# DeltaNet and a low-rank token mixer in one kernel: the low-rank products on smaller tiles of TensorE, with a new table of ranks

## The chip, the cores and the metric

The kernel runs on one core of a Trainium2 chip. The metric is the device time of one execution in microseconds (us); lower is better. The core has five engines with queues of their own: TensorE (PE in the profile; PEld is its weight load), VectorE (DVE), ScalarE (ACT), GpSimd (POOL) and SyncE (SP), which here only issues transfers.

## The reference

Two layers follow each other. The first is a delta-rule recurrence over 768 tokens for 4 batches and 8 heads of size 48. Its output, with the heads side by side (384 columns), is the x of the second, a mixer with a low-rank product over the tokens and a two-layer product over the channels.

```python
k_n = k / (np.linalg.norm(k, axis=-1, keepdims=True) + 1e-06)
for t in range(S):
    y[:, :, t] = np.einsum('bhd,bhde->bhe', q[:, :, t], state)
    v_old = np.einsum('bhde,bhd->bhe', state, kt)
    state = state + bt[:, :, :, None] * np.einsum('bhd,bhe->bhde', kt, vt - v_old)
...
xt = x.transpose(0, 2, 1)
h = xt @ U @ V
u = x + h.transpose(0, 2, 1)
ch = np.maximum(u @ w_ch1, 0.0) @ w_ch2
return (u + ch).astype(np.float32)
```

U is 768 x 32, V 32 x 768, w_ch1 384 x 1536, w_ch2 1536 x 384. U, V and the two weights come as 64-bit floats and are turned into 32-bit ones on the chip; everything else is fp32.

## The kernel before, in words

**The recurrence.** Each batch is cut in two units of 6 chunks of 64 tokens (units n = 0 to 7). For a unit, q and k are loaded and turned on TensorE (L646 with full 128x128 transposes, or L420 with 64x64 matmuls against the identity), multiplied with each other (L673), and a triangular system per chunk and head is solved: VectorE does a substitution (L758, L764) on blocks laid out by transposes (L749, L771), and TensorE joins the blocks (L814, L828, L854 to L875). The products L973 and L984 prepare a unit. Then `recur` goes through the chunks of a batch: L1022 applies the state, VectorE subtracts (z, L1035), L937 and L951 make the output y, which ScalarE copies to X (L921), and L1050 makes the change of the state, which VectorE adds (s, L1060). Each of these steps on TensorE is a group of eight small matmuls.

**The weights** are decoded on VectorE (L1155 to L1183) in 14 slices, two of them U and V, from staging space that lies partly in X and hs. V stands four times in v_sb, once in each quarter of the partitions.

**The mixer.** `front(b, i)` is called for each batch b and each third i of its tokens (256). For i = 0 it makes tt = U^T x (L1346): the six 128-token blocks of x are multiplied by U's blocks on four column tiles of 32, so that tt holds four partial sums of 384 columns in its four quarters of partitions; VectorE copies it out (L1352). For each i it then makes V^T tt (L1364), one 128x128 matmul of 384 columns for each 128-token block, which also adds up the four quarters; VectorE adds it to X (L1368), TensorE turns the result (L1387 or L420), and ScalarE copies it to ut (L1390). `wide(b, i)` holds the first product over the channels in six groups (`channels`, L1447, six matmuls of 256 columns), each with a relu on ScalarE (L1412), and the second as seven products of six matmuls (`narrow`, L1562), whose results VectorE gathers into X (L1487). The last batch makes its first product in another way (`quick`, L1251).

**The order of the work** is not written by hand. Every part is a generator that yields the operations it wants to do, with an estimated cost and a mode, and the keys it needs (`need`) or gives (`emitted`). `run` keeps a model of the engines' clocks and always emits next the operation that could start first, in case of a tie the one with the lower rank. The ranks are the table PLACES: "channels b0 i1 e4 84.16" is the rank of one part. An entry that ends in "quad 1" allows a part a second form. The instructions are emitted in that order; hardware waits are added for what they read and write.

**Modes.** "F" is a matmul on the full 128x128 array, "Q" four 64x64 tiles (QUADS), "T" column tiles of 32, "J" 32x32 tiles. A part with two forms takes "Q" only when its quad entry is there and the array is in that mode already. In the Q form a channel group takes both PSUM banks of `mix`, of which the full form takes one, and goes in two halves: `crossed` (L408) emits four 64x64 matmuls for two outputs, and between the halves `swap` has ScalarE read one column of each bank (L417). Two products of `narrow` can be paired in the same way.

The piece that makes the Q form:

```python
def crossed(jobs):
    for r, g in QUADS:
        to, w, x, start, stop = jobs[r]
        nc.tensor.matmul(
            to[half(g)], w[half(r), half(g)], x[half(r)],
            start=start, stop=stop, skip_group_check=True,
        )
```

Of the kernel before, what the change touches and what calls it, by code (L numbers as in the profile page):

```python
# [8 lines left out]
FP32 = mybir.dt.float32  # L9
# [6 lines left out]
L = 64  # L16
# [10 lines left out]
def kernel(  # L27
# [115 lines left out]
    add_up b0 i0 76.06; add_up b0 i1 10; add_up b0 i2 92; add_up b1 i0 94.5; add_up b1 i1 -57.95  # L143
    add_up b1 i2 13.5; add_up b2 i0 4.89; add_up b3 i0 119.12; add_up b3 i1 17.69; add_up b3 i2 2.95
    blocks n1 83.63; blocks n2 19.95; blocks n3 96.74; blocks n4 107.02; blocks n5 204.56; blocks n6 121.16
    blocks n7 126.66; both 73; channels b0 i0 e0 96.95; channels b0 i0 e1 105.6; channels b0 i0 e2 -27.57
    channels b0 i0 e3 129.38; channels b0 i0 e4 91.95; channels b0 i0 e5 71.15; channels b0 i1 e0 25
    channels b0 i1 e1 19.03; channels b0 i1 e2 34; channels b0 i1 e3 5.2; channels b0 i1 e4 84.16
    channels b0 i1 e5 30.5; channels b0 i2 e0 52; channels b0 i2 e1 46.94; channels b0 i2 e2 75.56
    channels b0 i2 e3 116.36; channels b0 i2 e4 51.09; channels b0 i2 e5 99.28; channels b1 i0 e0 113.65  # L150
    channels b1 i0 e1 91.5; channels b1 i0 e2 53.98; channels b1 i0 e3 100.61; channels b1 i0 e5 120.34
    channels b1 i1 e0 128.05; channels b1 i1 e1 30.85; channels b1 i1 e2 104.15; channels b1 i1 e3 58.65
    channels b1 i1 e4 15.5; channels b1 i1 e5 91.65; channels b1 i2 e0 118.43; channels b1 i2 e1 -2.08
    channels b1 i2 e2 73.28; channels b1 i2 e3 -8.98; channels b1 i2 e4 111.65; channels b1 i2 e5 32.87
    channels b2 i0 e0 38.24; channels b2 i0 e2 4.5; channels b2 i0 e3 127.92; channels b2 i0 e4 22.75
    channels b2 i0 e5 95.78; channels b2 i1 e0 274.53; channels b2 i1 e1 94; channels b2 i1 e2 97.16
    channels b2 i1 e3 91.59; channels b2 i1 e4 73; channels b2 i1 e5 1.09; channels b2 i2 e0 28.09
    channels b2 i2 e1 44.19; channels b2 i2 e2 57.06; channels b2 i2 e3 68.5; channels b2 i2 e4 73
    channels b2 i2 e5 9.5; copies 56.49; cut 75.73; diagonals n0 h0 19.22; diagonals n0 h1 62.5
    diagonals n1 h0 52; diagonals n2 h0 15.5; diagonals n2 h1 94.5; diagonals n3 h0 32; diagonals n3 h1 93.24  # L160
    diagonals n4 h0 7.5; diagonals n4 h1 95.58; diagonals n5 h0 33.96; diagonals n5 h1 27; diagonals n6 h0 92.63
    diagonals n6 h1 -0.5; diagonals n7 h0 88.94; diagonals n7 h1 69.62; first 30.4; front b0 i0 -7.49
    front b0 i0 quad 1; front b0 i1 75.5; front b0 i1 quad 1; front b0 i2 -10.38; front b1 i0 71.77
    front b1 i1 76; front b1 i1 quad 1; front b1 i2 73.06; front b2 i0 4.43; front b2 i0 quad 1; front b2 i1 12.82
    front b2 i1 quad 1; front b2 i2 68.32; front b2 i2 quad 1; front b3 i1 -1.47; front b3 i2 94.5
    gather b0 i0 h0 c0 77.72; gather b0 i0 h0 c1 16.74; gather b0 i0 h1 c0 -15; gather b0 i1 h0 c0 -18.11
    gather b0 i1 h0 c1 -19.16; gather b0 i1 h1 c0 111.34; gather b0 i1 h1 c1 99.53; gather b0 i2 h0 c0 109.5
    gather b0 i2 h0 c1 36.92; gather b0 i2 h1 c0 4.78; gather b0 i2 h1 c1 84.78; gather b1 i0 h0 c0 21.21
    gather b1 i0 h1 c0 79.5; gather b1 i0 h1 c1 103.91; gather b1 i1 h0 c0 92.5; gather b1 i1 h0 c1 122.8
    gather b1 i1 h1 c0 101.5; gather b1 i2 h1 c0 77.08; gather b1 i2 h1 c1 45; gather b2 i0 h0 c0 13.32  # L170
    gather b2 i0 h0 c1 82.99; gather b2 i0 h1 c0 124.83; gather b2 i0 h1 c1 3.53; gather b2 i1 h0 c0 80.62
    gather b2 i1 h0 c1 73.95; gather b2 i1 h1 c0 80.36; gather b2 i1 h1 c1 76.58; gather b2 i2 h0 c0 95.84
    gather b2 i2 h1 c0 25.35; gather b3 i0 h0 c0 2.88; gather b3 i0 h0 c1 113; gather b3 i0 h1 c1 113
    gather b3 i1 h0 c0 -4; gather b3 i1 h0 c1 23.12; gather b3 i1 h1 c0 44.69; gather b3 i1 h1 c1 28.1
    gather b3 i2 h0 c0 105.1; gather b3 i2 h0 c1 37.88; gather b3 i2 h1 c0 109.03; gather b3 i2 h1 c1 92.38
    grams n0 i0 54.5; grams n0 i1 5; grams n1 i0 -5.73; grams n1 i1 16.5; grams n2 i0 64.85; grams n2 i1 5.5
    grams n3 i0 10.25; grams n4 i0 140.55; grams n4 i1 0; grams n6 i1 103.46; grams n7 i0 120.26
    grams n7 i1 124.04; joins n0 h1 42; joins n1 h0 -10.78; joins n1 h1 90.6; joins n2 h0 46.2; joins n2 h1 -9.38
    joins n3 h0 18.36; joins n3 h1 -3; joins n4 h0 49.57; joins n4 h1 108.36; joins n5 h0 6.33; joins n5 h1 -4.95
    joins n6 h1 102.05; joins n7 h0 91.09; joins n7 h1 -26.22; last_sum b0 i0 107.65; last_sum b0 i1 -0.5  # L180
    last_sum b0 i2 58; last_sum b1 i0 6.24; last_sum b1 i1 90.99; last_sum b1 i2 72.32; last_sum b2 i0 -3.27
    last_sum b2 i1 94.5; last_sum b3 i1 76.04; last_sum b3 i2 90; load n0 namek halves(0,) -2.13
    load n0 namek halves(1,) 6.19; load n0 nameq halves(0,) 89.12; load n0 nameq halves(1,) 77.79
    load n0 namev halves(0,) 106; load n0 namez halves(0,) 113.97; load n0 namez halves(1,) 7.5
    load n1 namek halves(0,) 81.07; load n1 namek halves(1,) 73.91; load n1 nameq halves(0,) 43.57
    load n1 nameq halves(1,) 91.1; load n1 namev halves(0,) 27.89; load n1 namev halves(1,) 70.76
    load n1 namez halves(0,) 93.39; load n1 namez halves(1,) 5.01; load n2 namek halves(0, 1) 29.55
    load n2 nameq halves(0, 1) 67.61; load n2 namev halves(0, 1) 60.56; load n2 namez halves(0, 1) 107.23
    load n3 namek halves(0, 1) 11; load n3 nameq halves(0, 1) -4.84; load n3 namev halves(0, 1) 66.59
    load n3 namez halves(0, 1) 25.89; load n4 namek halves(0, 1) 65.35; load n4 nameq halves(0, 1) 24.5  # L190
    load n4 namev halves(0, 1) 81; load n4 namez halves(0, 1) 30.74; load n5 namek halves(0, 1) 109.5
    load n5 nameq halves(0, 1) 92; load n5 namev halves(0, 1) 38.85; load n5 namez halves(0, 1) -21.49
    load n6 namek halves(0, 1) 32.5; load n6 nameq halves(0, 1) 37.61; load n6 namev halves(0, 1) 7.15
    load n6 namez halves(0, 1) 62; load n7 namek halves(0, 1) 95; load n7 nameq halves(0, 1) 1.5
    load n7 namez halves(0, 1) 47.39; load_beta u0 45.5; load_beta u1 29.9; load_weights 107.15
    narrow b0 i0 e0 56.12; narrow b0 i0 e0 quad 1; narrow b0 i0 e1 123.3; narrow b0 i0 e2 71.6
    narrow b0 i0 e3 101.43; narrow b0 i1 e0 41.5; narrow b0 i1 e0 quad 1; narrow b0 i1 e2 81.41
    narrow b0 i1 e3 118.5; narrow b0 i1 e3 quad 1; narrow b0 i2 e0 92.51; narrow b0 i2 e1 88.93
    narrow b0 i2 e2 -54.32; narrow b0 i2 e2 quad 1; narrow b0 i2 e3 94.65; narrow b1 i0 e0 45.5
    narrow b1 i0 e0 quad 1; narrow b1 i0 e1 90.54; narrow b1 i0 e1 quad 1; narrow b1 i0 e2 16.95  # L200
    narrow b1 i0 e3 14.03; narrow b1 i1 e0 93.52; narrow b1 i1 e1 44.39; narrow b1 i1 e3 98
    narrow b1 i1 e3 quad 1; narrow b1 i2 e0 99.1; narrow b1 i2 e0 quad 1; narrow b1 i2 e1 30.56
    narrow b1 i2 e2 62; narrow b1 i2 e2 quad 1; narrow b1 i2 e3 0.76; narrow b2 i0 e0 108.5
    narrow b2 i0 e1 135.19; narrow b2 i0 e2 56.93; narrow b2 i0 e3 42.7; narrow b2 i1 e0 quad 1
    narrow b2 i1 e1 -11.39; narrow b2 i1 e2 109.47; narrow b2 i1 e2 quad 1; narrow b2 i1 e3 quad 1
    narrow b2 i2 e0 86.52; narrow b2 i2 e0 quad 1; narrow b2 i2 e1 92.56; narrow b2 i2 e2 106.1
    narrow b2 i2 e3 quad 1; narrow b3 i0 e0 95.5; narrow b3 i0 e1 66.42; narrow b3 i0 e1 quad 1
    narrow b3 i0 e2 24; narrow b3 i0 e2 quad 1; narrow b3 i0 e3 80.5; narrow b3 i1 e0 102.5; narrow b3 i1 e1 70.08
    narrow b3 i1 e2 1; narrow b3 i2 e0 48.87; narrow b3 i2 e1 58; narrow b3 i2 e1 quad 1; narrow b3 i2 e2 55.62
    narrow b3 i2 e2 quad 1; narrow b3 i2 e3 97.45; norms n0 68.5; norms n1 -53.8; norms n2 30.5; norms n3 110.41  # L210
# [1430 lines left out]
```

## Time and profile before

| | |
|---|---|
| median of 3 runs | 618.48 us (618.42 to 619.09) |
| span of the profiled execution | 612.3 us |
| what lies around the span (median less span) | 6.2 us |
| TensorE busy | 582.1 us, 10824 matmul records |
| VectorE busy | 417.3 us, 1000 instructions |
| ScalarE busy | 236.6 us |
| GpSimd busy | 98.4 us |
| U products start (L1346) | 109.8, 240.5, 377.6, 488.7 us |
| first matmul of the last batch's own first product (L1251) | 524.1 us |

The profile is one execution, seen from the first to the last instruction; its own time is the span and what lies around it, and by the median of the runs that is 618.5 us. An fp32 matmul leaves two records on TensorE, a transpose one. TensorE's matmuls overlap, so the mean length of one (243 ns for the small ones) is not its price: that is the length of a group in the chain of work divided by its matmuls. The clock of a stretch is the share of the full TensorE clock that was granted in it. Stages are told here from one U product to the next.

### The profile page before, as it was taken

To read this page: it belongs to the slowest core of one execution; us is meant where nothing else is said; L and a number is where in the kernel's file an instruction comes from. 1 tells how busy PE (TensorE), PEld (TensorE's weight loads), DVE (VectorE), ACT (ScalarE), POOL (GpSimd) and SP (SyncE) were. 2 spreads that over 40 slices of the span, in tenths; PEclk is the share of its full clock that TensorE was granted. 3 is DMA by queue.
4 is the path that set the end of the run, shared out by engine and by line. 5 is a ranking of instruction groups with operands and counts; after the bars stand their busy time and mean duration, and the time that the engine had idled before them with its cause. 6 is when DMAs were issued, how large, how long until landed. Compare 5 with 4: busy or idle time off the path is not lost.

```text
span 612.3 us, 24053 instructions
## 1 busy us (share of the span) xinstructions
PE 582.1 (95%) x10824; PEld 502.3 (82%) x10824; DVE 417.3 (68%) x1000; ACT 236.6 (39%) x466; POOL 98.4 (16%) x169
## 2 busy tenths in 40 slices
PE   4798887999999999999999999999999999999997
PEld 4788786688989987988889988978989889656997
DVE  5998899898899348988895888287843223332542
ACT  3645666255412652265218224253163220344000
POOL 8321050520004304110043002220010000000000
PEclk9655557799999999999999999999999999999999
DMA  9911686940006205200071002310000000000000
GB/s 142 163 42 55 209 193 169 137 130 19 3 28 98 67 4 91 61 16 3 4 123 42 16 16 53 74 42 4 28 3 3 29 2 1 26 2 0 16 36 27
DMA packets 63847, 33.31 MB, mean 54 GB/s; under 512 B 50816, under 2 KB 61824, under 8 KB 63744
## 3 DMA queue, kind: packets, MB, share of 16 engines
q1 hardware_dynamic: 56800, 23.21, 17.6%
q0 software_dynamic: 5344, 8.27, 6.5%
q8 instruction: 85, 1.39, 0.9%
q10 hardware_dynamic: 1600, 0.30, 0.3%
q14 instruction: 18, 0.15, 0.1%
HBM read 27.03 MB, written 4.72 MB: 52 GB/s over the span
## 4 chain that ended last, share of the span: by engine, by line
PE 83%; DVE 11%; issue 2%; ACT 2%; POOL 1%; DMA 1%; DVEq 0%; ACTq 0%; POOLq 0%
PE P L1562 25%; PE P L1447 24%; PE P L1251 7%; PE P L673 3%; PE P L408 3%; PE P L1364 2%; PE P L646 2%; PE P L1022 2%; PE P L973 2%; PE P L1050 2%; PE P L984 2%; PE P L951 2%; DVE prod L758 2%; PE P L937 2%; DVE xt L764 2%
## 5 line engine op out<-in xcount | busy, mean ns | idle before, releaser
L1447 PE MATMUL P<-ut,w_sb 128*128 128x256 f32 x648 | 151.6, 385 | 0.1
L1447 PEld LDWEIGHTS P<-ut,w_sb 128*128 128x128 f32 x648 | 119.4, 190 | 18.2 <-issue 1.2
L1562 PE MATMUL P<-w_sb,hs 128*128 128x192 f32 x468 | 82.4, 330 | 0.2 <-ACT hs L1412 0.2
L1562 PEld LDWEIGHTS P<-w_sb,hs 128*128 128x128 f32 x468 | 75.9, 190 | 2.0 <-ACT hs L1412 0.3
L764 DVE TENSOR_TENSOR xt<-xt,prod 128x112 f32<-128x112 f32 (+21 forms) x200 | 64.6, 323 | 6.9
L758 DVE TENSOR_TENSOR prod<-gs,xt 128x112 f32<-128x112 f32 (+21 forms) x200 | 64.0, 320 | 4.4
L1487 DVE TENSOR_TENSOR X<-X,P 128x192 f32<-128x192 f32 x84 | 29.3, 351 | 53.5 <-PE P L1562 50.7
L1412 ACT ACTIVATE hs<-P 128x512 f32<-128x512 f32 x54 | 32.3, 597 | 82.9 <-PE P L1447 73.6
L921 ACT COPY X<-P 64x192 f32<-64x192 f32 x96 | 30.0, 313 | 80.7 <-PE P L951 74.0
L1562 PE MATMUL P<-w_sb,S 128*128 128x192 f32 x264 | 45.9, 328 | 0.0
L1562 PEld LDWEIGHTS P<-w_sb,S 128*128 128x128 f32 x264 | 42.9, 190 | 1.2 <-DVE X L1487 0.6
L531 POOL DMA_DIRECT2D slot<-in_k_dram x44 | 29.1, 671 | 64.3 <-PE P L1050 64.2
L646 PE MATMUL P<-ident,slot 128*128 128x128 f32 x192 | 30.8, 309 | 8.2 <-DMA slot<-in_k_dram 8.1
L673 PE MATMUL P<-slot 48*64 48x64 f32 x1536 | 32.8, 243 | 4.8 <-ACT slot L660 4.8
L893 ACT COPY slot<-zz 32x384 f32<-32x384 f32 x64 | 32.5, 508 | 9.1 <-DVE zz L832 4.9
L673 PEld LDWEIGHTS P<-slot 48*64 48x64 f32 x1536 | 29.4, 155 | 7.9 <-ACT slot L660 6.0
L646 PEld LDWEIGHTS P<-ident,slot 128*128 128x128 f32 x192 | 25.0, 158 | 11.7 <-issue 8.7
L1251 PE MATMUL P<-slot,w_sb 128*128 128x384 f32 x96 | 33.2, 486 | 0.0
L1562 PE MATMUL P<-w_sb,slot 128*128 128x192 f32 x180 | 30.6, 327 | 0.9 <-DVE X L1487 0.9
L660 ACT COPY slot<-P 128x768 f32<-128x768 f32 x30 | 23.5, 796 | 20.1 <-PE P L646 18.0
L1562 PEld LDWEIGHTS P<-w_sb,slot 128*128 128x128 f32 x180 | 29.4, 190 | 2.0 <-DVE X L1487 1.5
L531 POOL DMA_DIRECT2D slot<-in_q_dram x32 | 21.0, 664 | 56.8 <-ACT X L921 40.5
(150 smaller groups left out, 935.9 us busy)
## 6 DMA issues: line engine op xcount, KB each, us to landing
out_dram<-X SPq DMA_DIRECT2D x22, 192.0 KB, 1.9
X<-in_moe_w_ch_dram SPq DMA_DIRECT2D x10, 384.0 KB, 3.9
wide<-in_moe_w_ch_dram SPq DMA_DIRECT2D x10, 384.0 KB, 4.4
slot<-in_k_dram SPq DMA_DIRECT2D x48, 72.0 KB, 4.8
slot<-in_k_dram POOLq DMA_DIRECT2D x44, 72.0 KB, 4.8
slot<-in_q_dram SPq DMA_DIRECT2D x32, 72.0 KB, 4.4
slot<-in_q_dram POOLq DMA_DIRECT2D x32, 72.0 KB, 4.7
slot<-in_v_dram SPq DMA_DIRECT2D x32, 72.0 KB, 3.4
```

What stands on the lines that cost most here:

```text
L531: queue.dma_start(out=t[half(1 - g if name == "z" else g), :, to, 0:D], in_=src[b, 4 * g + s, hf * UC * L : (hf + 1) * UC * L, :].rearrang ...
L646: nc.tensor.transpose(p_t[:, c // 3, c % 3], t[:, c, 2 * j : 2 * j + 2].rearrange("p s d -> p (s d)"), ident,)
L673: nc.tensor.matmul(p_g[half(g ^ (par * i)), par, c], kq[rows, c, j, 0, half(g)], kq[rows, c, j, i, half(g)], start=True, stop=True,)
L758: nc.vector.tensor_tensor(out=prod, in0=gb[:, :, j : j + 1, j + 1 :].to_broadcast([128, split, m, w]), in1=xb[:, :, 0:m, j : j + 1].to_bro ...
L764: nc.vector.tensor_tensor(out=xb[:, :, 0:m, j + 1 :], in0=xb[:, :, 0:m, j + 1 :], in1=prod, op=ALU.subtract,)
L893: nc.scalar.copy(pg[quarter(i), :, at, :, a : a + BK], cut(zc, h)[quarter(i)].rearrange("p r (c j) t -> p r c j t", j=2),)
L921: nc.scalar.copy(x[half(c % 2), c // 2, 4 * D * g : 4 * D * (g + 1)].rearrange("p (j r d) -> p r j d", r=2, d=D), states(p_y)[half(g)],)
L1251: nc.tensor.matmul(to, w, t, start=start, stop=stop, skip_group_check=True)
L1412: nc.scalar.activation(hs[:, fs[0] : fs[1] + 1 : fs[1] - fs[0]], p_f, ACTF.Relu)
L1447: nc.tensor.matmul(p_f[:, x], w(x, t), ut[:, t], start=(t == 0), stop=(t == KT - 1))
L1487: nc.vector.tensor_tensor(out=to, in0=to, in1=p, op=ALU.add)
L1562: nc.tensor.matmul(to, of[0], of[1], start=of[2], stop=of[3], skip_group_check=True)
```

## The change

U^T x goes on the four column tiles in another division: two tiles take the left half of the columns and two the right half, one of each pair the even token blocks and one the odd ones, so there are 12 matmuls of 192 columns and tt has 192 columns. In tt, the upper 64 partitions then hold two partial sums of the left half and the lower 64 those of the right. The V product follows that: for each token block four 64x64 tiles of 192 columns, over 64 rows each, in place of one 128x128 matmul of 384 columns. The addition to X reads its halves from two PSUM banks.

In the planner the modes and costs of the two operations are those of the new forms (U product 0.98 and 48 words, V product 0.66, "Q" and 32 words). New keys are needed: a load into a unit's space needs the last state product of the unit two before (`used`), the second copy of beta rows the first transposed betas, the copies of y to X the end of what was staged there (beta in batch 0; weight slices 12 and 13 in batch 1), and the first batch's relu slice 7, which was staged in hs.

PLACES is a new table: 607 entries in place of 511, 17 of them unchanged. It has 78 quad entries in place of 37; those of `channels` (35) are new. In the order of instructions that results, 14 of the 54 channel groups and 2 pairs of second products have the Q form, where it was none and 4; 170 changes of mode become 154.

```diff
     PLACES = """
...
-    channels b0 i0 e3 129.38; channels b0 i0 e4 91.95; channels b0 i0 e5 71.15; channels b0 i1 e0 25
...
+    turn n5 i1 j1 nameq 113.93; turn n5 i1 j1 nameq quad 1; turn n6 i0 j0 namek 94.9; turn n6 i0 j0 namek quad 1
...
-        yield need(("rec", n - 2), *[("x", b - 1, UC * hf + c) for c in range(UC)])
+        yield need(("rec", n - 2), ("used", n - 2), *[("x", b - 1, UC * hf + c) for c in range(UC)])
...
         rows = beta_rows
+        yield need(("betas", 0)) if u else []
...
         def put(c, y, p_y):
-            yield need(("stored", b - 2, c // 2)) if b > 1 else []
+            yield need(("stored", b - 2, c // 2)) if b > 1 else need(
+                ("beta", 1) if b == 0 else ("freed", W2 + 4) if c < 8 else ("weights", W2 + 5)
+            )
...
+                if cu == UC - 1:
+                    emitted(("used", n))
                 yield op("dve", dve(192), give=[("pair", xs)])
...
+            else:
+                emitted(("used", n))
...
         if i == 0:
-            o = yield op("pe", 1.3, "T", take="pair", words=24)
-            p_t = one(o)[:, 0:DM]
-            for c in range(NB):
-                nc.tensor.matmul(
-                    p_t[R * (c % 4) : R * (c % 4) + R], u_sb[:, c], x[:, c],
-                    start=(c < 4), stop=(c + 4 >= NB),
-                )
-            yield op("dve", dve(384), give=[("pair", o)])
-            tts[b] = mix.tile([128, DM], FP32, name="tt", bufs=1)
+            o = yield op("pe", 0.98, "T", take="pair", words=48)
+            p_t = one(o)[:, 0:HD]
+            for c in range(0, NB, 2):
+                for k in range(4):
+                    nc.tensor.matmul(
+                        p_t[quarter(k)], u_sb[:, c + k % 2],
+                        x[:, c + k % 2, HD * (k // 2) : HD * (k // 2) + HD],
+                        start=(c == 0), stop=(c + 2 == NB),
+                    )
+            yield op("dve", dve(HD), give=[("pair", o)])
+            tts[b] = mix.tile([128, HD], FP32, name="tt", bufs=1)
             nc.vector.tensor_copy(out=tts[b], in_=p_t)
...
-        o = yield op("pe", 1.3, "F", take="pair", words=8)
-        p_h = pair(o)[:, :, 0:DM]
+        o = yield op("pe", 0.66, "Q", take="pair", words=32)
+        p_h = pair(o)[:, :, 0 : NT * HD].rearrange("p r (m d) -> p r m d", m=NT)
         for m, c in enumerate(cs):
-            nc.tensor.matmul(
-                p_h[:, m], v_sb[:, c * 128 : (c + 1) * 128], tt, start=True, stop=True
-            )
+            for r, g in QUADS:
+                nc.tensor.matmul(
+                    p_h[half(g), r, m],
+                    v_sb[half(r), c * 128 + L * g : c * 128 + L * g + L],
+                    tt[half(r)],
+                    start=True,
+                    stop=True,
+                )
         yield op("dve", dve(768), give=[("pair", o)])
-        nc.vector.tensor_tensor(out=x[:, at], in0=x[:, at], in1=p_h, op=ALU.add)
+        to = x[:, at].rearrange("p m (r d) -> p r m d", r=2)
+        nc.vector.tensor_tensor(out=to, in0=to, in1=p_h, op=ALU.add)
...
         def relu(fs, ms, p_f):
+            yield need(("freed", W2 - 1)) if b == 0 else []
             yield op("act", act(2 * GT), give=[("mix", m) for m in ms])
```

## The prediction

> **What bounds the kernel now.** I read the page's head and slices first, then the busy time by stretch, then the chain of work in order of time, and last the timeline around one of the rare quarter-array products.
>
> ```profile
> span 612.3 us, 24053 instructions
> ...
> PE 582.1 (95%) x10824; PEld 502.3 (82%) x10824; DVE 417.3 (68%) x1000; ACT 236.6 (39%) x466; POOL 98.4 (16%) x169
> ...
> DVE  5998899898899348988895888287843223332542
> ...
> PEclk9655557799999999999999999999999999999999
> ...
> PE 83%; DVE 11%; issue 2%; ACT 2%; POOL 1%; DMA 1%; DVEq 0%; ACTq 0%; POOLq 0%
> ```
>
> TensorE is busy for 95% of the span and has 83% of the chain. The first 105 us are different: VectorE is at nine tenths, and TensorE runs at half clock.
>
> ```profile
> 75.00:90.00 15.00, 13.37 (x465) 12.32 (x469) 14.16 (x26) 9.75 (x21) 6.93 (x12) 0.56 0.80 195
> 90.00:105.00 15.00, 10.40 (x367) 8.86 (x364) 14.80 (x27) 9.84 (x17) 1.29 (x3) 0.84 0.78 194
> ...
> 150.00:200.00 50.00, 49.98 (x899) 45.40 (x899) 45.27 (x114) 15.42 (x31) 6.88 (x11) 1.00 0.23 41
> ...
> 350.00:400.00 50.00, 49.93 (x759) 43.34 (x758) 33.27 (x82) 16.93 (x35) 7.78 (x12) 1.00 0.20 44
> ```
>
> (Columns: stretch, length, then TensorE, weight loads, VectorE, ScalarE, GpSimd with counts, granted clock, DMA.) From 150 us on TensorE has no idle time and clock 1.00: what leaves its queue there leaves the total. Prices come from the chain in order of time (start, length, line, records; an fp32 matmul leaves two records, a transpose one):
>
> ```profile
> 240.48 1.42 PE P L1346 x12
> 241.89 1.49 PE P L1447 x6
> 243.38 1.29 PE P L1364 x4
> ...
> 300.50 0.99 PE P L408 x24
> ...
> 430.10 0.71 PE P L420 x48
> ...
> 494.89 1.30 PE P L1447 x6
> ```
>
> L1447 is 1.29 to 1.30 us inside a run of full-array work and 1.49 when it is the first after another tile shape: a change of shape costs 0.20 in this direction and 0.15 in the other (L673, x48: 0.86 after full-array work, 0.71 otherwise). I take 0.175 for each.
>
> **The change, part by part.** The profiled execution's span is 612.3 us; the median of the runs is 618.5, so 6.2 us lie around the span, and I keep these. The sum is made against 612.3 and 6.2 together, which is the median.
>
> *U^T x.* Before, 6 matmuls of 384 columns on four column tiles: 1.42 with its change of shape, 1.29 without, two rounds of 0.645 (L1364's matmul of the same 384 columns). After, 12 matmuls of 192 columns, three full rounds. L408 moves 12 quarter-array matmuls of 192 columns in 0.99, so three rounds are 0.98. Four times 0.31 is -1.2 us. The tt copy has half the columns (0.56 to about 0.35 on VectorE, four times); in the TensorE-bound stages this hides under the channel or product groups next in the queue.
>
> *V product.* Before, 2 matmuls of 384 columns, 1.29. After, 8 quarter-array matmuls, two rounds of 192: 0.65 by the same row. Twelve times 0.64 is -7.7 us. The addition to X keeps its 768 elements (L1368, 0.95): nothing.
>
> *New ranks.* They decide order and form. I compared the order in which the instructions of the two kernels stand. Matmul totals are equal but for forms: 14 of 54 channel groups (none before) and 2 pairs of the second product (4 before) are in quarter-array form. A form costs the same: 24 quarter matmuls of 256 columns are six rounds of 0.43, which six full ones take too. After the first U product 18 full transposes fewer, at 0.109 each (-2.0), stand against 48 quarter ones more, at 0.71 per 24 (L420: +1.4). Changes of shape there go from 139 to 125: -14 x 0.175 = -2.4.
>
> *Check of these prices.* I sum each stage of the queue (three channel matmuls 1.29, six second products 1.95, quick 0.645 a matmul, a recurrence group of eight 0.235, 24 products 0.71) from one U product to the next. Before this gives 129.7, 137.1, 108.3 and 35.5 us; the trace has 130.7, 137.1, 111.1 and 35.4 (U products at 109.8, 240.5, 377.6, 488.7, first quick matmul at 524.1). The prices hold. The changed order gives 132.7, 122.3, 122.6 and 21.1: 398.7 against 410.6, or -11.9. The last batch is the same list of matmuls in both.
>
> *Ahead of the first U product* VectorE sets the pace: 106.8 us of its work stand ahead of the first tt copy, which began at 112.6. The changed order puts 106.1 there. SP and GpSimd queue the same transfers; GpSimd's memset of xt moves ahead of four q loads, and three v loads behind the next memset, which waits for VectorE (L771, 27.6). Four loads took 2.6 us to issue and 3.5 to land, so these land near 36.4, where L610 read them at 36.6. Nothing, within a microsecond.
>
> *Waits written down.* Most hold a load, a copy out of PSUM or a relu behind work that stands far ahead: weights 7 and 12 are decoded at 92 and 140 us, before the first relu needs the one and the second batch's x the other. A load that now also waits for the last state product of the unit two before waited for that unit's outputs already; the next loads and stores stand behind it on SP and GpSimd, and only transposes of a later unit wait for them. Nothing; if the cover went, a load's 4.8 us to land would be seen.
>
> *What the quarter form adds.* Between the halves of such a group TensorE waits for a ScalarE read (L417). The timeline of one of the four that existed:
>
> ```profile
> 468.31 0.44 PE L1022 MATMUL P<-s,slot 48*64 48x48 f32 x12
> ...
> 468.65 0.16 ACT L417 COPY seen<-P 128x2 f32<-128x2 f32 x1 [2.48 <-PE P L408]
> 468.86 0.37 PEld L408 LDWEIGHTS P<-w_sb,hs 64*64 64x64 f32 x12
> ```
>
> From leaving the first half (468.31) to the second (468.86): 0.55, with two recurrence groups (0.47) in it, 0.08 open. Nine of the 14 have just two such groups there: about 1.0 in all. A quarter channel also takes both banks that full channels alternate in, so the relu before it (L1412, 0.60) must end first: at 371.5 TensorE left a channel and re-entered both banks 0.74 later, behind three groups. In seven places of the new order one or two groups stand there: 1.6 together. Bounds: 0 if all is covered, 14 x (0.68 + 0.75) = 20 if nothing is. I take 2.6, since I can count the cover.
>
> The Trainium skill, TensorEngine Tiling (Array Packing), Performance Considerations (PSUM Bottleneck), says that tiling speeds up TensorE but not the emptying of PSUM, which may become the limit. By it the sum would lie toward the upper bound, at 629; the four pairs in this trace, 0.08 open in the one shown, speak for the lower, near 611.
>
> *Stage after the first U product.* There VectorE is near. I sum VectorE's work from the first tt copy and TensorE's from the first U product up to the places where one needs the other: where TensorE reads the second batch's first z, its sum was 3.9 us ahead of VectorE's before and is 0.3 now; at the first matmul (L854) on unit 3's solved blocks it was 7.1 and is 2.9. In addition the first V product has no filler behind the tt copy, and a quarter channel follows the first turned x with ScalarE's 0.80 copy in between. Bounds 0 (before showed no TensorE idling in 150 to 200) and 3.6 (all the slack lost). I take 2.0. Instruction fetches: TensorE's records go from 21648 to 23004, five more of the 256-record packets of which queue q8 moved 85; TensorE stood once for 1.3 us (L872, "issue") between two of these. I take 0.3 of 0 to 1.3.
>
> Sum: 618.5 - 11.9 + 2.6 + 2.0 + 0.3 = 611.5.
>
> **Rivals.**
> *All covered.* The new waits hide, and the 2.8 us that stage three lost before (111.1 against 108.3) may be saved too: 606.6, at best 603.8. For: TensorE idled under 1 us in most stretches. Against: 14 new halting points.
>
> *VectorE binds the first mixed stage.* It has 116.7 us of work between first and second tt copy, 108.3 before, in 129.4 us. With the same 21.1 idle it needs 137.8, where my stage has 134.7: 614.6. For: the slack of 0.3. Against: part of that idling was waiting for TensorE.
>
> *Slower: quarter channels held by both banks.* Place: L408's channel groups, their L417 read and L1412 relu. Price up to 1.43 each, 629 at full. From 0.7 us open per group (618.5 less 608.9, over 14) the kernel is slower. Against: the order puts recurrence work in each gap. For: nine gaps are covered by 0.47 only, and ScalarE's 0.31 copies may stand ahead of the read.
>
> *The tiles don't overlap.* If V's eight matmuls ran one after another (0.33 each) they would cost 2.6, not 0.65: 611.5 + 23 = 635. L408's 24 records in 0.99 speak against it.
>
> **How the numbers follow.** Chances: forecast 0.43, all covered 0.27, VectorE-bound 0.11, slower by held banks 0.12, no overlap 0.02, no measurable change 0.05 (several of the costs at half). A difference of 0.2% (1.2 us) is about what a measurement can tell from no change. Faster gets 0.43 + 0.27 + 0.11 = 0.81; same 0.05; slower 0.14. The predicted time is the forecast's, 611.5. The range 604.5 to 619 takes in the first three cases and leaves out the slower ones and a little below.
>
> **What would show it.** U groups of 0.98 us and V groups of 0.65 in the chain; TensorE near 570 us busy; L417 with 16 copies and under 0.3 us idle of TensorE around each; TensorE still without idle in 150 to 200. Wrong if L408 or the groups next to it wait on ScalarE for more than 0.7 each, if the first U product comes after 113 us, or if V's groups take over 1 us.

## The result: faster by 3 to 4 us, where 7 were forecast

The changed kernel has a median of 614.53 us (611.88 to 617.45, 12 runs), the kernel before 618.22 us (615.05 to 619.09, 12 runs). The ratio is 0.9955, with an interval of 0.9934 to 0.9976. The forecast was 611.5 us: the direction and the range held, the size did not. By the medians the gain is 3.7 us, by the ratio 2.8 (1.5 to 4.1), where 7.0 were forecast. That the range held says little: it ended at 619 and so took in a kernel that had not changed at all (618.5).

The first lines of the page of the changed kernel: span, busy time of the engines, slices of VectorE and of the granted clock, and the chain by engine.

```profile
span 610.2 us, 25422 instructions
...
PE 571.3 (94%) x11502; PEld 497.0 (81%) x11502; DVE 417.4 (68%) x1000; ACT 237.1 (39%) x478; POOL 98.4 (16%) x169
...
DVE  4999897898998528898887388869852124332542
...
PEclk9976556799999999999999999999999999999999
...
PE 82%; DVE 10%; ACT 3%; issue 3%; DMA 1%; ACTq 0%; DVEq 0%
```

TensorE is busy for 10.8 us less, as its lists of matmuls said it would be (near 570). But the span is only 2.1 us shorter, and this execution took 611.88 us, 1.7 more than its span. In every later profile it is 1.6 to 2.0 (617.0 for a span of 615.3, 609.64 for 607.9). So the profiled execution of before, with a span of 612.3, took about 614.0 by estimate. It was a quick one, and the 6.2 us "around the span" were mostly the distance from it to the median. I therefore cut the spans in two, and profiled the kernel before once more.

| us | first U product starts | from there to the end | U to U, U to U, U to U, U to quick, quick to end |
|---|---|---|---|
| before | 109.7 | 502.6 | 130.7, 137.1, 111.1, 35.3, 88.4 |
| before, second profile | 113.6 | 501.7 | 130.1, 137.1, 110.8, 35.3, 88.4 |
| changed | 115.3 | 494.9 | 135.7, 124.4, 125.3, 21.1, 88.4 |
| changed, second profile | 118.4 | 496.6 | 136.7, 124.6, 125.8, 21.1, 88.4 |

From the first U product on the change gains 6.4 us by the means of the two profiles (7.7 by the first ones); the forecast's terms for that part sum to 7.0. Ahead of it the changed kernel is later by 5.2. Single profiles are rough here, since the start alone varies by some 4 us (the two parts together give a gain of 1.2, where the runs give 2.8 to 3.7), but this is the only part in which time was lost.

The same stretches of time as before, now of the changed kernel (stretch, length, then TensorE, weight loads, VectorE, ScalarE, GpSimd with counts, granted clock, DMA share, GB/s):

```profile
75.00:90.00 15.00, 12.47 (x400) 11.44 (x400) 13.72 (x25) 9.37 (x21) 6.79 (x11) 0.50 0.77 186
90.00:105.00 15.00, 10.47 (x286) 9.73 (x290) 11.56 (x18) 7.39 (x12) 1.87 (x5) 0.55 0.80 157
150.00:200.00 50.00, 49.27 (x1065) 43.70 (x1064) 45.25 (x115) 17.34 (x35) 7.68 (x13) 1.00 0.20 37
350.00:400.00 50.00, 48.84 (x998) 41.85 (x1000) 39.79 (x105) 15.98 (x38) 13.70 (x23) 1.00 0.35 68
```

Between 90 and 105 us VectorE, which set the pace there, has 11.56 us of work where it had 14.80 (the second profiles have 11.01 and 12.72): it waits. For what, the changed kernel's chain of work shows (start, length, line, records):

```profile
94.34 0.42 PE P L964 x15
94.76 3.52 issue
98.28 0.24 PE P L964
98.52 0.38 PE P L1077 x14
```

TensorE stops for 3.52 us in the middle of a group of eight small matmuls, after 15 of its 16 records, and waits for nothing that the profile shows. The group is the state applied to q (L964, L951 before), and the recurrence behind it, on VectorE too, stands with it. In the trace, the packets of instructions on queue q8 (90 of 16 KB in the page's list of DMA queues) start at 81.9, 87.6, 95.3 and 99.4 us, and the one of 95.3 takes 1.60 us: TensorE went on only behind that one, at 98.28. I read this as TensorE having run out of instructions. All nine profiles with this order of TensorE's early work bear it out: each has the stop at this one record, 0.8 to 4.1 us long, and each goes on 1.35 to 1.65 us after the end of the last packet on q8.

The prices of the forecast are in the same chain, around the second U product:

```profile
251.11 1.11 PE P L1378 x24
252.22 0.86 PE P L698 x48
253.08 0.65 PE P L1398 x16
...
261.09 0.81 PE P L1398 x16
```

The U product takes 1.11 with its change of shape, the V product 0.65 in quarter-array company and 0.81 behind full-array work; 0.98 and 0.65 without changes were forecast.

### The profile page after: what moved, and what is told of

Its sections match the earlier page's. It is cut to its first block, busy times and chain, and to the rows that moved or that the text cites. A ratio compares the mean times of both kernels' runs of the same rounds, so it can differ in the third digit from the quotient of the medians.

```text
span 610.2 us, 25422 instructions
## 1 busy us (share of the span) xinstructions
PE 571.3 (94%) x11502; PEld 497.0 (81%) x11502; DVE 417.4 (68%) x1000; ACT 237.1 (39%) x478; POOL 98.4 (16%) x169
## 4 chain that ended last, share of the span: by engine, by line
PE 82%; DVE 10%; ACT 3%; issue 3%; DMA 1%; ACTq 0%; DVEq 0%
PE P L1602 26%; PE P L1487 18%; PE P L432 8%; PE P L1282 7%; PE P L698 3%; PE P L671 2%; PE P L1049 2%; PE P L978 2%; PE P L1011 2%; PE P L1000 2%; PE P L964 2%; PE P L1077 1%; DVE xt L789 1%; DVE prod L783 1%; PE P L853 1%
## 5 line engine op out<-in xcount | busy, mean ns | idle before, releaser
L1487 PE MATMUL P<-ut,w_sb 128*128 128x256 f32 x480 | 111.4, 385 | 0.4
L1487 PEld LDWEIGHTS P<-ut,w_sb 128*128 128x128 f32 x480 | 88.9, 190 | 12.9 <-ACT hs L1452 1.1
L1602 PE MATMUL P<-w_sb,hs 128*128 128x192 f32 x492 | 87.2, 331 | 0.1
L1602 PEld LDWEIGHTS P<-w_sb,hs 128*128 128x128 f32 x492 | 79.5, 190 | 2.7 <-ACT hs L1452 0.8
L1602 PE MATMUL P<-w_sb,S 128*128 128x192 f32 x288 | 49.7, 328 | 0.0
L1602 PEld LDWEIGHTS P<-w_sb,S 128*128 128x128 f32 x288 | 46.7, 190 | 0.4 <-issue 0.3
L432 PE MATMUL P<-ut,w_sb 64*64 64x256 f32 x672 | 45.1, 383 | 1.8 <-ACT ut L1429 0.9
L671 PE MATMUL P<-ident,slot 128*128 128x128 f32 x180 | 29.5, 315 | 11.0 <-DMA slot<-in_k_dram 9.4
L555 POOL DMA_DIRECT2D slot<-in_v_dram x32 | 21.2, 669 | 70.7 <-PE P L671 63.0
```

Source lines behind the costliest of these rows:

```text
L432: nc.tensor.matmul(to[half(g)], w[half(r), half(g)], x[half(r)], start=start, stop=stop, skip_group_check=True,)
L555: queue.dma_start(out=t[half(1 - g if name == "z" else g), :, to, 0:D], in_=src[b, 4 * g + s, hf * UC * L : (hf + 1) * UC * L, :].rearrang ...
L671: nc.tensor.transpose(p_t[:, c // 3, c % 3], t[:, c, 2 * j : 2 * j + 2].rearrange("p s d -> p (s d)"), ident,)
L1487: nc.tensor.matmul(p_f[:, x], w(x, t), ut[:, t], start=(t == 0), stop=(t == KT - 1))
L1602: nc.tensor.matmul(to, of[0], of[1], start=of[2], stop=of[3], skip_group_check=True)
```

## The experiments

**Theory A**, formed after the result: from the first U product on, all went as forecast; the loss is in the start, and comes from the order in which the new ranks let SyncE and GpSimd issue the transfers: a packet of instructions for TensorE comes late behind them. **Rival R1:** the start only varies from execution to execution. **Rival R2:** the quarter-array channel groups hold both banks, and cost what is missing. **Rival R3:** the smaller tiles of U and V gain less than forecast.

Most kernels below take the order of work from a written list in place of the planner, so that order and forms can be changed apart. Each has one of the two kernels' orders, or a mix:

```diff
     def run():
-        while waits or woken:
...
+        todo = []
+        for t in ORDER.split():
+            t, _, bank = t.partition("b")
+            todo.append((NAMES[int(t.rstrip("q"))], t.endswith("q"), int(bank) if bank else None))
...
+            for place, k in enumerate(left):
+                u, quad, bank = todo[k]
```

The waits that were written down need no run. With these alone, and with the old ranks and forms, the order of the instructions is that of the kernel before on all five engines.

**The kernel before, a second profile.** Its edit is none.

> The kernel before once more, for a second profile. Theory A (the changed order of transfers and work ahead of the first U product holds TensorE up, mostly in two waits for instructions, 3.5 and 1.4 us): the first U product starts again near 110 us and the rest takes 502.5 us. Theory B (the start of any of these kernels varies by several us from execution to execution, with the granted clock, and the order has no part in it): the first U product may start anywhere from 109 to 116 us, the rest again takes 502.5 us within 1 us.

It took 617.0 us; the first U product came at 113.6, and from there it took 501.7. The start varies by some 4 us, the rest by 1. This profile also has a stop for instructions near the same place, 1.4 us at 96.2, which the first one has not.

**The forms of U and V alone, in the order of before.** The diff is that of the change in `front`, with ORDER from the kernel before:

```diff
-            o = yield op("pe", 1.3, "T", take="pair", words=24)
...
+            o = yield op("pe", 0.98, "T", take="pair", words=48)
...
-        o = yield op("pe", 1.3, "F", take="pair", words=8)
...
+        o = yield op("pe", 0.66, "Q", take="pair", words=32)
```

> The instructions in the order of the kernel before, with only the U and V products in their new forms. Both theories: after the first U product 8.9 us less for the products and 15 more changes of shape at 0.175, so -6.3 us: 496.2 in place of 502.5. Theory A: the start is that of before, about 110 us, total ratio near 0.990. Theory B: the start falls anywhere from 109 to 116.

It took 617.89 us, ratio 1.0039 (1.0012 to 1.0066): a little slower, where a gain of 1% was expected. First U product at 111.1, 503.6 from there. The stages are 135.0, 137.0, 109.1 and 34.1. Of the 7.4 us that are missing against the expectation, about 6 lie in the first stage, which by the prices (0.31 and three times 0.64 less, three changes of shape more) falls by 1.7 and rose by 4.3. The trace has two stops for instructions there:

```profile
125.88 0.55 PE P L876 x41
126.42 1.94 issue
128.36 0.24 PE P L876 x6
```

The other is 0.85 long, at 160.2 us, and for 3.5 us, from 129.0, the clock was 0.5. In the later stages the gain is 3.3 us for nine V products and three U products. Less 0.31 for each U product, a V product gains 0.3 there, not 0.64: most stand between full-array groups, and 12 of the 15 added changes of shape lie in these stages (2.1 us by the price). The order decides what the form is worth. Of the 6 us in the first stage the two stops are 2.8; what the half clock has of the rest was not separated.

**The new order alone, with the old forms of U and V.** The reverse of the diff above, with ORDER from the changed kernel.

> The instructions in the order of the changed kernel, with the U and V products in their old forms. After the first U product both theories expect the 494.9 us of the changed kernel plus 8.9 and 3 more changes of shape, 504.3, which is 2 us more than before: the new order with its 14 quarter channels costs there a little more than it saves. Theory A: the first U product starts near 115 us, so the total is about 7 us above before, ratio 1.011. Theory B: the start is as in any other run, ratio near 1.003.

It took 623.43 us, ratio 1.0109 (1.0071 to 1.0147). First U product at 116.7, and 503.2 from there; the stop of the start is there too, 3.8 us long. Against the changed kernel, which has the same order, this tells what the forms are worth in it: 503.2 less 494.9 is 8.3 us, where 8.9 were forecast; against the second profile of the changed kernel, 496.6, it is 6.6. The chain of this kernel around the second U product, to be held against the lines above:

```profile
255.63 1.41 PE P L1401 x12
257.04 0.86 PE P L722 x48
257.90 1.49 PE P L1419 x4
```

U goes from 1.41 to 1.11, V with its change of shape from 1.49 to 0.65. R3 falls in the new order and holds in the old one.

**The order of before up to the first U product, the new one behind it.** The edit is ORDER alone: the operations of the kernel before until the first U product, then those of the changed kernel which are left.

> The changed kernel, but everything that the kernel before issues ahead of its first U product is issued in that old order, and the rest in the new one. Theory A: the first U product starts near 110 us, the rest takes 495 us, and the total is 7 to 8 us below before, ratio 0.988, below the changed kernel's 0.9955. Theory B: no better than the changed kernel within the spread, ratio 0.9955, with a start anywhere from 109 to 116 us.

It took 622.87 us, ratio 1.0099 (1.0072 to 1.0127), where a gain was expected. The first U product came at 114.4, and the first stage then took 142.7 instead of 135.7, with a stop for instructions of 2.2 us at 134.3 and half clock from 121.7 to 125.1 and from 135.4 to 142.2. Both of Theory A's figures, 110 us and 0.988, were missed: the start came late with the old order too, and without a long stop at 94. The mix does not separate the start from what follows, since the two orders have different work left over at the first U product. So the run does not support Theory A, and its slow first stage does not decide against it.

**The loads of units 2 and 3 cut to one chunk of six, in both kernels.** These leave out five sixths of q, k and v of the second batch, which are loaded from about 80 us on.

```diff
+                cn = 1 if n in (2, 3) else UC
                 queue.dma_start(
-                    out=t[half(1 - g if name == "z" else g), :, to, 0:D],
-                    in_=src[b, 4 * g + s, hf * UC * L : (hf + 1) * UC * L, :].rearrange(
+                    out=t[half(1 - g if name == "z" else g), 0:cn, to, 0:D],
+                    in_=src[b, 4 * g + s, hf * UC * L : (hf * UC + cn) * L, :].rearrange(
```

> The changed kernel with one chunk of six in each load of units 2 and 3 (q, k, z and v: the rest of these units' data is left out, so this is a measurement of time alone). The order of all instructions stays. Theory A1 (TensorE's instruction packets arrive late because the transfer engines are full of the loads of units 2 and 3 ahead of the first U product): the waits named issue at 94.8 and 112 us (3.5 and 1.4) are gone, the first U product starts near 110 us, and the total is 4 to 5 us below the changed kernel, ratio to before about 0.987. Theory A2 (the waits come from the rate at which TensorE's queue consumes small instructions there, whatever else is moved): they stay, ratio near 0.9955.

> The kernel before with the same loads cut to one chunk of six (units 2 and 3, the rest left out). Theory A1: the kernel before has no long wait for instructions ahead of its first U product, so little is gained, at most 1 us, ratio 0.998 to 1. Theory A2: nothing.

The changed kernel took 611.78 us so, ratio 0.9909 (0.9876 to 0.9941); the kernel before 614.82, ratio 0.9962 (0.9939 to 0.9984). The stop of 3.5 us is down to 0.8. So it has to do with the loads. But the first U product came only at 114.0, not near 110, and the kernel before gains by it too, 2.9 us where at most 1 was expected; the difference between the two kernels stays at 3.0 us. Smaller loads help both kernels; they don't explain the difference alone.

**The changed kernel with the transfers in the order of before.** On TensorE, VectorE and ScalarE nothing moves. SyncE's first 62 queue operations and GpSimd's first 64 (its memsets and masks among them) are emitted in the order of the kernel before. SyncE's two orders differ in two places, in the first loads of all (shown further down) and for unit 2. There the edit is (z is a second load from k, 72 KB like the others):

```diff
-load n2 z, load n2 z
+load n2 k, load n2 k
...
-load n2 k, weights, weights, load n2 k, load n2 q, load n2 q, load n2 q, load n2 q
+load n2 q, load n2 q, load n2 q, load n2 q, weights, weights, load n2 z, load n2 z
```

> The changed kernel in which only the two queues that issue transfers, SyncE's first 62 and GpSimd's first 64 operations, stand in the order of the kernel before; TensorE's, VectorE's and ScalarE's instructions stand as in the changed kernel. Theory A1, in the form that the order of the transfers is what made the packets late: the first U product starts near 111 us, the total is 3 to 5 us below the changed kernel, ratio about 0.988. If the waits come from TensorE's own new order instead: first U product near 115 to 116 us, ratio near 0.9955 as for the changed kernel.

It took 610.03 us (608.67 to 611.68, 4 runs), ratio 0.9894 (0.9852 to 0.9936): as far below the kernel before as was forecast, and less than both kernels. The first U product came at 112.6, and 495.3 us followed. In the timeline of SyncE (start, length, line, what it issues), first that of the kernel before and then that of the changed one:

```profile
84.90 3.56 SPq L531 DMA_DIRECT2D slot<-in_q_dram  x4
88.56 1.22 SPq L1132 DMA_DIRECT2D wide<-in_moe_w_ch_dram  x2
```

```profile
87.93 1.52 SPq L1163 DMA_DIRECT2D wide<-in_moe_w_ch_dram  x2
...
90.21 3.78 SPq L555 DMA_DIRECT2D slot<-in_q_dram  x4
```

The four q loads, which stood ahead of the weight slices, now stand behind them, and are issued until 94.0; TensorE stops at 94.8.

**The channel groups of the changed kernel all in full form.** In ORDER the 14 marks for the quarter form are left out:

```diff
-    (channels b0 i0 e0, quarter form), ...
+    (channels b0 i0 e0, full form), ...
```

> The changed kernel with its 14 quarter channel groups in the full form, in the same places. Shape changes after the first U product rise from 125 to 159, 34 x 0.175 = 6.0 us; the waits on banks and on ScalarE's read, which the prediction put at 2.6, go. Expected after the first U product 494.9 + 6.0 - 2.6 = 498.3, ratio to before about 1.001. If the quarter channels held TensorE by both banks as the slower rival had it (over 0.7 us each, 9.8 in all), this kernel is the faster one: about 491, ratio 0.989.

It took 624.37 us, ratio 1.0135 (1.0087 to 1.0184), and 506.4 from the first U product, where 498.3 was expected: 11.5 more than in the first profile of the quarter form, 9.8 more than in the second. Changes of shape went up from 125 to 159 there, 6.0 us at 0.175 each. For the rest, the longest waits of TensorE between 118 and 520 us, of this kernel and then of the changed one (columns: line, what ended the wait, us in total, times, longest):

```profile
PE P L1073 <- DVE s L1113: 1.8, 4, 0.6
PE P L1422 <- DVE tt L1409: 1.5, 3, 0.5
```

```profile
PE P L432 <- ACT ut L1429: 0.9, 1, 0.9
PE P L432 <- ACT hs L1452: 0.9, 3, 0.3
```

All of that view's waits come to 11.6 us here and to 5.0 in the changed kernel. The order was made for the quarter forms, and without them its small waits grow. R2 falls: the wait for a relu before a quarter group is at most 0.3 long.

**The changed kernel again, and one transfer queue at a time.** These four shared a chip. The edits are none, SyncE's 62 operations alone, GpSimd's 64 alone, and both. The single queues are not quite alone: where SyncE goes back, four of GpSimd's operations change places too, and where GpSimd goes back, six of SyncE's.

```diff
-    transfers: SyncE in the new order, GpSimd in the new order
+    transfers: SyncE in the order of before, GpSimd in the new order
```

> The changed kernel a second time, for a second profile and a wider sample beside the next three. Theory A (the order of the transfers makes one packet of instructions late): the profile again has a TensorE wait of 3.2 to 3.9 us without a cause in the trace at 93 to 97 us, the first U product comes at 114.5 to 117, the rest takes 494 to 496, ratio 0.993 to 0.998. Rival N (the start is drawn anew in every execution, and the order of the transfers has nothing to do with it): the wait is as likely absent as present, and the first U product comes anywhere from 110 to 117.

> The changed kernel with only SyncE's first 62 queue operations in the order of the kernel before; GpSimd's stay in the new order. Theory S (SyncE's queue is the cause: there the new order sends the z and q loads of unit 2 in another sequence and two 384 KB weight slices ahead of four of them): the wait of 3.2 to 3.9 us falls to under 1, first U product at 111 to 114, ratio 0.988 to 0.992. Theory P (GpSimd's queue is the cause: there loads of unit 2 stand ahead of the masks of unit 1, and those of unit 3 come in another sequence): nothing changes, first U product at 114.5 to 117, ratio 0.993 to 0.998.

> The changed kernel with only GpSimd's first 64 queue operations in the order of the kernel before; SyncE's stay in the new order. Theory S: nothing changes, the wait of 3.2 to 3.9 us stays, first U product at 114.5 to 117, ratio 0.993 to 0.998. Theory P: the wait falls to under 1 us, first U product at 111 to 114, ratio 0.988 to 0.992. If both halves only do part (ratio 0.991 to 0.995 each), it is the amount that is in flight at the time, not one queue.

> The changed kernel with the first operations of both transfer queues in the order of the kernel before, a second time, for its profile and interval. Theory A: no wait above 1.5 us at 90 to 100, first U product at 111 to 114, rest 494 to 496, ratio 0.986 to 0.992, below that of the changed kernel in the same runs by 0.004 or more. Rival N: the ratio lies within 0.002 of the changed kernel's, and a wait above 3 us is as likely as not.

| changed kernel with | median us | ratio to before | first U product | stop at 93 to 102 us |
|---|---|---|---|---|
| nothing else | 615.32 | 0.9940 (0.9914 to 0.9967) | 118.4 | 4.1 |
| GpSimd's order of before | 612.81 | 0.9937 (0.9900 to 0.9974) | 116.7 | 2.7 |
| SyncE's order of before | 611.49 | 0.9890 (0.9836 to 0.9944) | 115.8 | 1.1 |
| both | 611.15 | 0.9884 (0.9834 to 0.9933) | 112.8 | 2.4 |

TensorE's waits from 90 to 116 us, of the changed kernel's second profile, of the one with SyncE's order of before, and of the second profile of the kernel before:

```profile
PE P L964 <- issue: 4.1, 1, 4.1
```

```profile
PE P L1024 <- issue: 1.4, 1, 1.4
PE P L988 <- issue: 1.1, 1, 1.1
```

```profile
PE P L951 <- issue: 1.4, 1, 1.4
```

By the ratios SyncE's queue is the one that matters: its old order alone gives 0.9890 and both give 0.9884, where GpSimd's gives 0.9937, against 0.9940 with nothing else. By the medians it is 3.8 of the 4.2 us between the first and the last row; GpSimd's median is 2.5 lower too, but its ten runs go from 610.40 to 619.02. Two of the rows have only four runs. By single profiles it is less clean: the changed kernel's second one starts later and stops longer than Theory A expected, with both queues in the old order the second profile still has a stop of 2.4, where under 1.5 was expected, and with SyncE's alone the first U product came at 115.8, later than expected. Rival N, by which the wait would come and go at random, falls for the new order, where it is there in four profiles of four. R1 holds in part: one and the same kernel varies by 3 to 4 us in its start, but giving back the transfers alone moved the time.

The stop goes with the distance between two packets of instructions on q8, by the trace:

```
kernel                                 packet to packet us   TensorE stopped us
before                                 85.4 to 90.2: 4.7     none
before, again                          87.2 to 94.5: 7.3     1.4
changed                                87.6 to 95.3: 7.7     3.5
changed, again                         90.7 to 99.0: 8.3     4.1
new order, old forms                   87.1 to 95.2: 8.1     3.8
new order, full channels               88.3 to 96.1: 7.8     3.2
GpSimd's transfers as before           89.4 to 97.2: 7.8     2.7
both transfer queues as before, again  86.8 to 93.6: 6.8     2.4
SyncE's transfers as before            88.4 to 93.4: 5.0     1.1
both transfer queues as before         86.1 to 91.2: 5.1     0.8
smaller loads                          88.8 to 94.6: 5.8     0.8
```

With SyncE's new order the distance is 7.7 to 8.3 in all five profiles with full loads, with its old one 4.7 to 7.3: a late packet is not peculiar to the new order, but the new order has it each time. The DMA engines are not clearly busier in the new order: from 90 to 105 us their share is 0.80 and 0.96 in the two profiles of the changed kernel, 0.78 and 0.83 in those of the kernel before. Why the new order lets a packet start later is not settled; it could be what stands ahead of it on single engines, which was not measured.

The late packet is not all that the transfers do. In the first loads, behind four of k, SyncE issues q and k by fours in turn in the kernel before, and eight of q, then eight of k, in the changed one. The second entry of its timeline, of the kernel before and then of the changed one:

```profile
3.89 2.65 SPq L531 DMA_DIRECT2D slot<-in_q_dram  x4
```

```profile
3.97 5.83 SPq L555 DMA_DIRECT2D slot<-in_q_dram  x8
```

TensorE's waits from 12 to 25 us, of the changed kernel:

```profile
PE P L671 <- DMA slot<-in_k_dram: 2.2, 1, 2.2
PE P L671 <- DMA X<-in_moe_U_dram: 1.5, 1, 1.5
```

With SyncE's new order such waits for transfers come to 3.7 to 6.2 us there in all five profiles with full loads, with its old order to 1.7 at most. The group in which TensorE stops later begins at 94.1, 97.4, 93.8 and 95.1 us in the four profiles of the new order, and at 92.7 and 93.4 with both queues in the old one. So by the means some 2 us of the 3.9 by which the first U product then comes earlier are there ahead of the stop, and another 2 are the shorter stop. Both places went back together in every run, so what each costs by itself was not measured, and that the early waits make the first 2 us is argued.

## Why the prediction was right on one part and wrong on another

- *What failed* is the step "Ahead of the first U product": "Nothing, within a microsecond". It counted VectorE's work (106.8 and 106.1 us, the lengths added up), and that this stays the same is right. But the lengths overlap: up to its first tt copy VectorE is busy for 97.6 and 98.4 us in the two profiles of before and 98.2 and 98.5 in those of the changed kernel, and stands idle for 14.9 and 18.0 there, 19.2 and 22.1 here. The step put nothing down for this idling, which is where the time went. It followed four v loads that moved on GpSimd at 27 to 37 us. It took it that SyncE queues the same transfers, and did not look at what the new ranks do to their order there, at 4 to 14 us and at 85 to 94, nor at the packets of instructions that share the DMA engines with them. Measured, the four profiles of the new order with its own transfers have the first U product at 115.3, 116.1, 116.7 and 118.4, those which begin in the order of before (the kernel before twice, with smaller loads, the forms alone, the mixed order) at 109.7 to 114.4: 116.6 against 111.9 in the mean, 4.7 us. Giving back the old order of the transfers takes 4.2 us off the time, by the medians of all runs (614.8, 22 runs; 610.6, 8 runs): TensorE waits for the first loads, and later for a late packet. That the order of the transfers costs this is shown; how it divides between the two places is open. With the 4.2 put in, the forecast would have been 611.5 + 4.2 = 615.7; the two series of the changed kernel have 614.53 and 615.32. This is an account made afterwards, since the 4.2 was measured on this kernel.
- *Instruction fetches* were costed at 0.3 of 0 to 1.3 us, by one stop of 1.3 in the trace of before. The term looked only at how many packets there are; one stop in the start is 3.2 to 4.1. Behind the first U product it did no harm: TensorE waits 0.8 for instructions there in the first profile of the changed kernel, 1.3 in that of before.
- *U^T x and V product*: -8.9 forecast, -8.3 measured (same order, old forms against new), -6.6 with the second profile of the changed kernel.
- *New ranks and what they add*, from the first U product on: -3.0 for forms and changes of shape, +4.9 for waits, +1.9 in all. Measured with the old forms: 503.2 against 502.6 and 501.7, +1.1. The sum was right; its parts were not measured one by one.
- *The quarter form's waits*: 2.6 forecast. In the whole span TensorE's matmuls of L432 wait 0.9 us for ScalarE's relu, in three places, and its weight loads, which overlap matmuls, another 2.1 in six; the read at the halves (L441) holds the group behind it once, for 0.3. So the term was too large by about half. The rule of the Trainium skill that was weighed here (TensorEngine Tiling (Array Packing), Performance Considerations, PSUM Bottleneck), by which emptying PSUM may become the limit of tiled products, is not seen in the channel groups: the matmuls' waits are under 0.1 a group in the mean. But these groups were priced the same in both forms, so they say little of a tiled product that is faster.
- *Stage after the first U product*: 2.0 were put down. It took 135.7 where the sum of its work was 132.7. The 0.80 copy ahead of the first quarter channel shows as a wait of 0.92, the tt copy as one of 0.52. VectorE does not bind it: that rival gave 137.8 by itself.
- *The baseline*: the 6.2 us "around the span" are 1.7. This did no harm to the difference, since both sums used it, but it hid that the trace of before was that of a quick start (109.7), so a start of 113 and more was no alarm by itself.
- Of the signs named ahead, the products' prices, TensorE's 571.3 us busy and the short waits at the halves came as told; TensorE without idle in 150 to 200 came nearly (49.27 of 50 us busy). The one that was to show it wrong came too: the first U product after 113 us. But the second profile of the kernel before has it at 113.6, so the sign was set too tight.

## What to carry to other kernels

When a change draws the order of the work anew, the transfer queues are to be compared line by line too, in every stretch in which the DMA engines are near full: TensorE's own instructions come through them, and a kernel with many small matmuls can stop in the middle of a group. What a quarter-array form is worth depends on the shape of its neighbours: the same V product gained 0.5 to 0.6 us in one order (6.6 or 8.3 less 1.2 for U, over 12) and 0.3 in the later stages of the other. And a span should be held against two or three profiles before a step is costed at nothing, where the start alone moves by 4 us.

## What the runs showed of the hardware that I had not expected

TensorE stands for up to 4.1 us behind a late packet of instructions, while loads are queued beside it, and with no mark in the profile but "issue". Cutting the loads, or sending the same loads in another order, brings it to 0.8 to 2.7. With the changed kernel's order the wait comes at one and the same record each time, and ends 1.35 to 1.65 us after the packet.

The granted clock does not tell how long the start takes. This is a stretch of the second profile of the changed kernel:

```profile
90.00:105.00 15.00, 8.86 (x294) 8.08 (x296) 11.01 (x18) 6.75 (x14) 4.68 (x8) 1.00 0.96 148
```

It had the full clock up to 118.7 us by the records, where the first profile of the same kernel had half of it from 52 to 103 and again from 110. Yet its first U product came later, at 118.4 against 115.3. What is longer in the second profile are the waits for the first loads and for the late packet, 5.2 and 4.1 us against 3.7 and 3.5.
